# Unordered scatters, weight casts issued turn by turn, and two additions moved from VectorE to TensorE

## The chip, the cores and the metric

The kernel runs on one core of a Trainium2 chip. The metric is the device time of one execution in microseconds (us). Each core has five engines with in-order instruction streams: TensorE (PE; its weight loads are listed as PEld), VectorE (DVE), ScalarE (ACT), GpSimd (POOL) and SyncE (SP). Here SP issues the plain DMAs, POOL the casting and the indirect ones. Data live in DRAM, in SBUF (128 partitions) and in PSUM, the only place that TensorE writes.

## The reference

Two stages. First, a gated linear recurrence with a complex state over 768 steps, for 4 batches and 8 heads of 48 dimensions; its output is then fed, regrouped as 3072 tokens of 384 numbers, to a mixture of eight experts of which each token uses one.

```python
mag = np.sqrt(a_re * a_re + a_im * a_im)
scale = np.minimum(mag, 0.999) / (mag + 1e-06)
a_re_n, a_im_n = (a_re * scale, a_im * scale)
for t in range(S):
    new_re = ar * S_re - ai * S_im          # ar, ai: a_re_n, a_im_n of step t
    new_im = ar * S_im + ai * S_re
    S_re, S_im = (new_re + kv, new_im)      # kv: outer product of k and v of step t
    y[:, :, t] = np.einsum('bhd,bhde->bhe', q[:, :, t], S_re)

logits = x @ w_gate + modality_bias[modality_id]
e_idx = np.argmax(logits, axis=1)           # gate_w: softmax weight of e_idx
for e in range(E):
    mask = e_idx == e
    h = np.maximum(x[mask] @ w1[e], 0.0)
    out[mask] = gate_w[mask, None] * (h @ w2[e])
```

## The kernel before

The sequence is cut into 8 pieces of 96 steps. Four batches x eight heads x eight pieces are 256 rows, handled in two rounds (r = 0, 1) of 128 rows, one row to a partition.

**`elem(r)`** makes what depends on the gates alone. It walks the 96 steps of all 128 pieces backwards, in 12 chunks of 8 steps (c = 11 down to 0). The product of the gates from a step to the end of its piece is the tile `e`. One step is a multiplication on DVE (`x`, L143) and an addition on DVE (`e`, L150) that gives the next `e`; the eight steps of a chunk depend on one another. Between these steps, the list `beside` places pieces of two generators:

- `modulus` (for the chunk two further on): two loads `ab` (a_re, a_im), their squares on ACT (`sq`, L69), the sum of the two squares on DVE (`m`, L72), then Ln, Exp and a Copy on ACT (`m`, `g`, L73 to L76), and the product `g` on DVE (L78). `gates` then makes the scaled gates `an` (DVE L85, ACT L86, L87).
- `hats` (for the chunk just done): the squares of `e` on ACT (`sqe`, L97), their sum on DVE (`me`, L100), Ln and Exp on ACT (L101, L102), the product `qc` on DVE (L104), the product `Qh` on DVE (L107), eight transposes on TensorE (`tq`, L111) that ACT copies to `QT` (L112), and the product of `e` and `kc` on DVE (L114), which goes to DRAM as `kh`.

**`units(r)`** is the matmul part: 16 units a round (8 pieces x 2 batches). A unit loads `KW` (from `kh`) and `V`, transposes (`tk` L177, copied to `KT`), multiplies `wp` (L184, float32, masked into `KW` on DVE, L185), transposes the decayed state (`tz` L207, copied to `Zs` on ACT), multiplies `py` (L219, L223), computes the logits (`lg_ps` L237) and writes the rows of x as bf16. POOL zeroes the padding of `V` and `KT` for each unit (L170, L173), and the load of `V` is queued on SP behind that zeroing.

`elem(0)` runs alone; then `units(0)` and `elem(1)` are interleaved piece by piece; then `units(1)` runs alone. The framework that lowers the program reorders each engine's instructions by its own estimate of when they are ready; from then on each engine runs its list in order.

**`cast_weights`** issues 16 DMAs on POOL (L289, L290) at the start of the program. Each reads one expert's w1 or w2 as float32 (1.57 MB) and writes a bf16 copy of it to DRAM.

**`moe_sorted`** sorts the tokens by expert and handles tiles of 256 slots, each of one expert: 12 tiles at least, and as many of 7 more as the counts need. For each tile, `fetch` loads the expert's two bf16 weight arrays (SP; `w1t`, `w2t`, three buffers each) and gathers the token rows with two indirect DMAs on POOL (`xg`, L449, six buffers); `turn` transposes them (`xg_ps` L457, copied by DVE to `xgT`); `up` multiplies (`h_ps` L469, evacuated in turn by DVE L471 and ACT L473); `down` multiplies (`y_ps` L481), scales the result into `y_sb` (ACT L484 and DVE L486, four buffers) and writes it to the token rows of `out` with two indirect DMAs on POOL (the scatters, L487). The framework takes two scatters to the same tensor as a write after a write, so that each waits until the one before has landed.

Of the kernel before, what the change touches and what calls it, by code (L numbers as in the profile page):

```python
# [19 lines left out]
ET = mybir.EngineType  # L20


def gate_loop(nc, ctx, tc, cpool, ident, identb, q, k, v, a_re, a_im, wgp, x_rows, lg):


    B, H, S, D = q.shape
    L = 96
    G = S // L
    P = 128
# [4 lines left out]
    T = 8  # L34
# [5 lines left out]
    ps = ctx.enter_context(tc.psum_pool(name="aps", bufs=1))  # L40
# [19 lines left out]

    for_round = {}

    def modulus(r, c, box):

        ab = st.tile([P, 2, T, D], F32, name="ab", bufs=3)
        nc.sync.dma_start(out=ab[:, 0], in_=rows(a_re, r, c))
        nc.sync.dma_start(out=ab[:, 1], in_=rows(a_im, r, c))
        sq = st.tile([P, 2, T, D], F32, name="sq")
        nc.scalar.activation(sq[:], ab[:], Act.Square)  # L69
        yield  # L70
        m = st.tile([P, T, D], F32, name="m", bufs=3)
        nc.vector.tensor_tensor(m[:], sq[:, 0], sq[:, 1], Alu.add)  # L72
# [17 lines left out]
    def hats(r, c, e, QT):  # L90

        qc = st.tile([P, T, D], F32, name="qc")
        kc = st.tile([P, T, D], F32, name="kc")
        nc.sync.dma_start(out=qc[:], in_=rows(q, r, c))
        nc.sync.dma_start(out=kc[:], in_=rows(k, r, c))
        sq = st.tile([P, T, 2, D], F32, name="sqe", tag="sq")
        nc.scalar.activation(sq[:], e[:], Act.Square)  # L97
        yield
        m = st.tile([P, T, D], F32, name="me", tag="m", bufs=3)
        nc.vector.tensor_tensor(m[:], sq[:, :, 0], sq[:, :, 1], Alu.add)  # L100
        nc.scalar.activation(m[:], m[:], Act.Ln)  # L101
# [5 lines left out]
        nc.vector.tensor_tensor(Qh[:], e[:], both(qc), Alu.mult)  # L107
        for t4 in range(0, T, 4):
            tp = ps.tile([C, 4, P], F32, name="tq", tag="tp", bufs=2)
            for i in range(4):  # L110
                nc.tensor.transpose(tp[:, i, :], Qh[:, t4 + i].rearrange("p c d -> p (c d)"), ident[:])  # L111
            nc.scalar.copy(QT[:, :, c * T + t4:c * T + t4 + 4], tp.rearrange("c t p -> c p t"))  # L112
        yield
        nc.vector.tensor_tensor(e[:], e[:], both(kc), Alu.mult)  # L114
        nc.sync.dma_start(out=kh[r, :, c * T:(c + 1) * T], in_=e.rearrange("p t c d -> p t (c d)"))

    def elem(r):

        QT = qt.tile([C, P, L], F32, name="QT", bufs=2)
        for_round[r] = QT  # L120
        last = NCH - 1
        E = {last: st.tile([P, T, 2, D], F32, name="e", bufs=3)}
        nc.vector.memset(E[last][:, T - 1, 0, :], 1.0)
        nc.vector.memset(E[last][:, T - 1, 1, :], 0.0)
        cl = un.tile([P, 2, D], F32, name="cl", bufs=1)
        box = {}
        for c in (last, last - 1):
            for _ in modulus(r, c, box):
                pass
        gates(last, box)  # L130
        for c in range(last, -2, -1):
            hs = hats(r, c + 1, E.pop(c + 1), QT) if c < last else iter(())
            ms = modulus(r, c - 2, box) if c > 1 else iter(())
            next(hs, None)
            next(ms, None)
            beside = [None, hs, ms, hs, hs, ms, hs, ms]
            if c >= 0:
                an = box.pop(c)
                if c:
                    E[c - 1] = st.tile([P, T, 2, D], F32, name="e", bufs=3)  # L140
                for i in range(T - 1, -1, -1):
                    x = st.tile([P, 2, 2, D], F32, name="x")
                    nc.vector.tensor_tensor(x[:], E[c][:, i, :, None, :].broadcast_to([P, 2, 2, D]), an[:, i].rearrange("p (u w) d -> p u w d", u=2), Alu.mult)  # L143
# [6 lines left out]
                    nc.vector.tensor_tensor(to, x[:, 0], x[:, 1], Alu.add)  # L150
# [132 lines left out]
def cast_weights(nc, moe_w1, moe_w2):  # L283

    E, Dt, F = moe_w1.shape
    w1b = nc.dram_tensor("w1b", (E, 128, Dt // 128, F), BF16, kind="Internal").ap()
    w2b = nc.dram_tensor("w2b", (E, 128, F // 128, Dt), BF16, kind="Internal").ap()
    for e in range(E):
        nc.gpsimd.dma_start(out=w1b[e], in_=moe_w1[e].rearrange("(k p) f -> p k f", p=128))  # L289
        nc.gpsimd.dma_start(out=w2b[e], in_=moe_w2[e].rearrange("(c p) d -> p c d", p=128))  # L290
    return w1b, w2b


def moe_sorted(nc, ctx, tc, cpool, identb, lg, x_rows, w1b, w2b, moe_modality_id, moe_modality_bias, out):

    N, Dt = out.shape
# [140 lines left out]
    ids = mp.tile([128, NH], U32, name="ids")  # L437
# [38 lines left out]
    def down(i, w2t, hT):  # L476
        for s in range(HS):
            c = i * HS + s
# [3 lines left out]
            y_sb = fp.tile([128, Dt], F32, name="y_sb", bufs=4)  # L482
            if s % 2 == 0:
                nc.scalar.activation(y_sb[:], y_ps[:], Act.Copy, scale=inv[:, 1, c:c + 1])  # L484
            else:
                nc.vector.tensor_scalar(y_sb[:], y_ps[:], inv[:, 1, c:c + 1], None, Alu.mult)  # L486
            nc.gpsimd.indirect_dma_start(out=out, out_offset=bass.IndirectOffsetOnAxis(ap=ids[:, c:c + 1], axis=0), in_=y_sb[:], in_offset=None, bounds_check=N - 1, oob_is_err=False)  # L487


    got = fetch(0)  # L490
# [18 lines left out]
def kernel(  # L509
# [14 lines left out]
    nc = tc.nc  # L524
# [19 lines left out]
    w1b, w2b = cast_weights(nc, moe_w1, moe_w2)  # L544
    with ExitStack() as gstack:
        gate_loop(nc, gstack, tc, cpool, ident, identb, q, k, v, a_re, a_im, wgp, x_rows, lg)
    moe_sorted(nc, ctx, tc, cpool, identb, lg, x_rows, w1b, w2b, moe_modality_id, moe_modality_bias, out)


# [28 lines left out]
```

## Time and profile before

| what | us |
|---|---|
| median of three timed runs (612.57, 619.71, 619.93) | 619.71 |
| the profiled execution's own time | 614.6 |
| its span | 612.7 |
| TensorE busy (matmul), of the span | 397.7 |
| VectorE busy, of the span | 354.4 |
| ScalarE busy, of the span | 266.7 |
| GpSimd busy, of the span | 82.7 |

The mean granted TensorE clock of the profiled execution is 0.851. A profile line of a timeline gives start (us), length (us), engine, line, operation, the tile written and the tiles read, shape and count; in square brackets stands the idle time of that engine before it and what ended it. A float32 matmul of the program appears as two MATMUL records (512 products `wp` are 1024 records), a transpose as one.

### The profile page before, as it was taken

The numbers are of one execution on the slowest core, as the hardware profiler recorded it, in microseconds if no ns is written. First come the engines' busy times: TensorE is split into PE (matmuls) and PEld (weight loads), VectorE is DVE, ScalarE is ACT, GpSimd is POOL, SyncE is SP. The second block draws the span as 40 slices with busy tenths as digits, with TensorE's granted clock in tenths as the row PEclk, the third lists the DMA queues.
The fourth block names the chain that finished last, engine by engine and source line by source line (L and its number), as shares of the span: only waits on it lengthen the run. The fifth ranks groups of instructions, "written<-read, shape, count | busy, mean of one in ns | idle before, by whom it ended". The sixth has DMA issues, their size and how long they took to land. (4 is left out here: it accounts for less than half of the span.)

```text
span 612.7 us, 10055 instructions
## 1 busy us (share of the span) xinstructions
PE 397.7 (65%) x3656; PEld 292.1 (48%) x3656; DVE 354.4 (58%) x884; ACT 266.7 (44%) x597; POOL 82.7 (13%) x144
## 2 busy tenths in 40 slices
PE   0022122129799978987987999999914695876670
PEld 0011011117566656665656767776604574654450
DVE  1899999988876587588871444444365142232120
ACT  3556756475745574476652444444410031211120
POOL 5112000000000000000000000000000343435322
PEclk9999999999755685588996999999955599887886
DMA  9999998365652364353525445444217177765610
GB/s 201 234 243 267 261 254 218 116 175 117 172 151 74 93 159 127 87 154 99 134 70 114 88 93 105 91 98 99 50 12 305 32 269 254 255 230 184 206 53 28
DMA packets 108405, 91.49 MB, mean 149 GB/s; under 512 B 73342, under 2 KB 97314, under 8 KB 108352
## 3 DMA queue, kind: packets, MB, share of 16 engines
q1 hardware_dynamic: 93920, 70.94, 41.7%
q0 software_dynamic: 14432, 19.86, 15.7%
q8 instruction: 31, 0.51, 0.4%
q14 instruction: 22, 0.18, 0.1%
HBM read 86.75 MB, written 29.59 MB: 190 GB/s over the span
## 5 line engine op out<-in xcount | busy, mean ns | idle before, releaser
L111 PE MATMUL tq<-ident,Qh 128*96 128x128 f32 x192 | 42.9, 390 | 119.2 <-DVE Qh L107 119.2
L111 PEld LDWEIGHTS tq<-ident,Qh 128*96 128x96 f32 x192 | 31.3, 180 | 128.2 <-ACT g L76 62.0
L219 PE MATMUL py<-KW,V 96*64 96x192 f32 x512 | 88.9, 378 | 0.0
L185 DVE TENSOR_TENSOR KW<-wp,mask 96x384 f32<-96x384 f32 x64 | 35.3, 553 | 78.5 <-PE wp L184 67.0
L143 DVE TENSOR_TENSOR x<-e,an 128x192 f32<-128x192 f32 x192 | 67.7, 353 | 2.5
L184 PE MATMUL wp<-QT,KT 96*64 96x96 f32 x1024 | 65.8, 287 | 0.8 <-ACT KT L178 0.5
L184 PEld LDWEIGHTS wp<-QT,KT 96*64 96x64 f32 x1024 | 58.5, 165 | 5.6 <-ACT KT L178 4.3
L469 PE MATMUL h_ps<-xgT,w1t 128*128 128x256 bf16 x312 | 42.6, 296 | 25.2 <-DVE hT L471 22.0
L473 ACT ACTIVATE hT<-h_ps 128x512 bf16<-128x512 f32 x26 | 15.5, 597 | 97.5 <-PE h_ps L469 97.5
L150 DVE TENSOR_TENSOR e<-x 128x96 f32<-128x96 f32 x190 | 48.0, 253 | 2.7
L469 PEld LDWEIGHTS <-w1t 128*128 128x128 bf16 x312 | 32.8, 105 | 33.3 <-issue 26.3
L173 POOL MEMSET KT<- 96x256 f32 x32 | 10.9, 365 | 275.0 <-PE wp L184 275.0
L223 PE MATMUL py<-QT,Zs 96*48 96x96 f32 x448 | 37.5, 272 | 14.1 <-ACT Zs L209 14.1
L177 PE MATMUL tk<-ident,KW 96*96 96x96 f32 x256 | 40.1, 298 | 9.4 <-DMA KW<-kh 8.9
L219 PEld LDWEIGHTS py<-KW,V 96*64 96x64 f32 x512 | 39.6, 154 | 10.4 <-issue 2.4
L486 DVE TENSOR_SCALAR y_sb<-y_ps,inv 128x384 f32<-128x384 f32 x13 | 8.0, 617 | 60.9 <-DMA out_dram<-y_sb,ids 48.0
L112 ACT COPY QT<-tq 96x512 f32<-96x512 f32 x48 | 27.5, 582 | 34.9 <-PE tq L111 34.7
L481 PE MATMUL y_ps<-w2t,hT 128*128 128x384 bf16 x208 | 40.5, 353 | 0.0
L223 PEld LDWEIGHTS py<-QT,Zs 96*48 96x48 f32 x448 | 26.7, 136 | 26.9 <-ACT Zs L209 22.7
L209 ACT COPY Zs<-tz 96x512 f32<-96x512 f32 x28 | 16.3, 582 | 48.5 <-PE tz L207 48.5
L177 PEld LDWEIGHTS tk<-ident,KW 96*96 96x96 f32 x256 | 28.5, 154 | 17.6 <-issue 10.4
L178 ACT COPY KT<-tk 96x384 f32<-96x384 f32 x64 | 29.2, 477 | 16.9 <-PE tk L177 16.1
(120 smaller groups left out, 700.6 us busy)
## 6 DMA issues: line engine op xcount, KB each, us to landing
w1t<-w1b SPq DMA_DIRECT2D x13, 768.0 KB, 5.0
w2t<-w2b SPq DMA_DIRECT2D x13, 768.0 KB, 5.5
kh<-e SPq DMA_DIRECT2D x24, 384.0 KB, 2.9
KW<-kh SPq DMA_DIRECT2D x32, 288.0 KB, 3.7
w1b<-in_moe_w_dram POOLq DMA_DIRECT2D x8, 768.0 KB, 43.8
w2b<-in_moe_w_dram POOLq DMA_DIRECT2D x8, 768.0 KB, 46.4
cB<-c_scr SPq DMA_DIRECT2D x56, 96.0 KB, 3.4
ab<-in_a_re_dram SPq DMA_DIRECT2D x24, 192.0 KB, 5.3
```

The source lines that it names most:

```text
L111: nc.tensor.transpose(tp[:, i, :], Qh[:, t4 + i].rearrange("p c d -> p (c d)"), ident[:])
L112: nc.scalar.copy(QT[:, :, c * T + t4:c * T + t4 + 4], tp.rearrange("c t p -> c p t"))
L143: nc.vector.tensor_tensor(x[:], E[c][:, i, :, None, :].broadcast_to([P, 2, 2, D]), an[:, i].rearrange("p (u w) d -> p u w d", u=2), Alu.mult)
L150: nc.vector.tensor_tensor(to, x[:, 0], x[:, 1], Alu.add)
L177: nc.tensor.transpose(tp[:, i, :], KW[:, h4 + i, 0:C], ident[:L, :L])
L178: nc.scalar.copy(KT[:, h4:h4 + 4, 0:L], tp[:])
L184: nc.tensor.matmul(wp[u * 64:(u + 1) * 64, i, :], KT[:, h4 + i, u * 64:(u + 1) * 64], QT[:, p, :], start=True, stop=True)
L185: nc.vector.tensor_tensor(KW[:, h4:h4 + 4, C:], wp[0:L], mask[:, None, :].broadcast_to([L, 4, L]), Alu.mult)
L219: nc.tensor.matmul(py[u * 64:(u + 1) * 64, i, :], V[:, 2 * j + u, :], KW[:, 2 * j + u, :], start=True, stop=(g == 0))
L223: nc.tensor.matmul(py[u * 64:u * 64 + D, i, C:], Zs[:, j, u * 64:u * 64 + D], QT[:, p, :], start=False, stop=True)
L469: nc.tensor.matmul(h_ps[:, f, :], w1t[:, k, ff * 128:(ff + 1) * 128], xgT[:, k, :], start=(k == 0), stop=(k == KD - 1))
L481: nc.tensor.matmul(y_ps[:], hT[:, f, s * 128:(s + 1) * 128], w2t[:, f, :], start=(f == 0), stop=(f == NF - 1))
```

## The change

Three edits.

1. **Sums on TensorE.** The two additions L72 and L100 go. In their place a function `total` adds the two halves of the squares with two accumulating float32 matmuls against the 128x128 identity, into a PSUM tile of 128x384 that shares its two buffers with `wp` (tag "wp"). The Ln on ACT then reads PSUM in place of SBUF.
2. **Casts turn by turn.** The 16 casts are kept in a list. `elem` issues one of them at the end of a chunk, with a dependency on the last addition of that chunk on DVE: ten in round 0 (c = 9 to 0), six in round 1 (c = 11 to 6). They stay on POOL.
3. **Scatters.** Each scatter to `out` is declared independent of the other scatters.

```diff
+    def total(x, y):
+        out = ps.tile([P, T, D], F32, name="total", tag="wp", bufs=2)
+        nc.tensor.matmul(out[:], ident[:], x, start=True, stop=False)
+        nc.tensor.matmul(out[:], ident[:], y, start=False, stop=True)
+        return out[:]
...
         m = st.tile([P, T, D], F32, name="m", bufs=3)
-        nc.vector.tensor_tensor(m[:], sq[:, 0], sq[:, 1], Alu.add)
-        nc.scalar.activation(m[:], m[:], Act.Ln, scale=1.0 / (0.999 * 0.999))
+        nc.scalar.activation(m[:], total(sq[:, 0], sq[:, 1]), Act.Ln, scale=1.0 / (0.999 * 0.999))
...
         m = st.tile([P, T, D], F32, name="me", tag="m", bufs=3)
-        nc.vector.tensor_tensor(m[:], sq[:, :, 0], sq[:, :, 1], Alu.add)
-        nc.scalar.activation(m[:], m[:], Act.Ln)
+        nc.scalar.activation(m[:], total(sq[:, :, 0], sq[:, :, 1]), Act.Ln)
...
-                    nc.vector.tensor_tensor(to, x[:, 0], x[:, 1], Alu.add)
+                    done = nc.vector.tensor_tensor(to, x[:, 0], x[:, 1], Alu.add)
+                if casts and (r or c < last - 1):
+                    cast = casts.pop(0)()
+                    tc.add_manual_dep(cast.ins, done.ins.name, ...)
...
+    casts = []
     for e in range(E):
-        nc.gpsimd.dma_start(out=w1b[e], in_=moe_w1[e].rearrange("(k p) f -> p k f", p=128))
-        nc.gpsimd.dma_start(out=w2b[e], in_=moe_w2[e].rearrange("(c p) d -> p c d", p=128))
+        casts.append(lambda e=e: nc.gpsimd.dma_start(out=w1b[e], in_=...))
+        casts.append(lambda e=e: nc.gpsimd.dma_start(out=w2b[e], in_=...))
...
-            nc.gpsimd.indirect_dma_start(out=out, out_offset=..., in_=y_sb[:], ...)
+            sc = nc.gpsimd.indirect_dma_start(out=out, out_offset=..., in_=y_sb[:], ...)
+            tc.declare_no_dep(sc.ins, group="scatter", reason="rows of different tokens")
+            tc.add_to_no_dep_group("scatter", sc.ins)
```

The order of the instructions changes with it. On DVE, one chunk of `elem(0)` from the first step on, before (the numbers tell one buffer of a tile from another):

```order
L143 TENSOR_TENSOR x_260<-e_191,an_194 128x192
L100 TENSOR_TENSOR me_269<-sqe_252 128x384
L150 TENSOR_TENSOR e_191<-x_260 128x96
L72 TENSOR_TENSOR m_276<-sq_257 128x384
L143 TENSOR_TENSOR x_267<-e_191,an_194 128x192
L150 TENSOR_TENSOR e_191<-x_267 128x96
L104 TENSOR_TENSOR qc_248<-qc_248,me_269 128x384
L143 TENSOR_TENSOR x_274<-e_191,an_194 128x192
L107 TENSOR_TENSOR Qh_289<-e_144,qc_248 128x768
L150 TENSOR_TENSOR e_191<-x_274 128x96
L78 SCALAR_TENSOR_TENSOR g_280<-m_276,g_280 128x384
```

The same stretch of a chunk on DVE now:

```order
L148 TENSOR_TENSOR x_473<-e_399,an_402 128x192
L155 TENSOR_TENSOR e_399<-x_473 128x96
L148 TENSOR_TENSOR x_480<-e_399,an_402 128x192
L155 TENSOR_TENSOR e_399<-x_480 128x96
L148 TENSOR_TENSOR x_489<-e_399,an_402 128x192
L155 TENSOR_TENSOR e_399<-x_489 128x96
L148 TENSOR_TENSOR x_500<-e_399,an_402 128x192
L109 TENSOR_TENSOR qc_461<-qc_461,me_482 128x384
L155 TENSOR_TENSOR e_399<-x_500 128x96
L112 TENSOR_TENSOR Qh_506<-e_326,qc_461 128x768
L148 TENSOR_TENSOR x_504<-e_399,an_402 128x192
L84 SCALAR_TENSOR_TENSOR g_497<-m_491,g_497 128x384
```

The two additions are gone; `qc` now stands behind three whole steps and the `x` of a fourth, where it stood behind two steps. In both, the gates `an` of the next chunk stand ahead of the first row.

On TensorE, in the interleaved stage, from the transposes `tz` of a unit to its first logits, before:

```order
L207 MATMUL tz_1536<-ident_58,Z_1492 96x128 x4
L223 MATMUL py_1546<-QT_106,Zs_1541 48x96 x2
L219 MATMUL py_1546<-KW_1333,V_1334 64x192 x2
L223 MATMUL py_1546<-QT_106,Zs_1541 48x96 x2
L223 MATMUL py_1558<-QT_106,Zs_1541 48x96 x2
L237 MATMUL lg_ps_1406<-yT_1544,wgp_66 32x96 x2
```

The same place of a unit now (`sqe` and `sq` are the squares of `e` and of the gates):

```order
L216 MATMUL tz_1870<-ident_58,Z_1826 96x128 x4
L66 MATMUL total_1944<-sqe_1926,ident_58 128x384
L67 MATMUL total_1944<-sqe_1926,ident_58 128x384
L232 MATMUL py_1880<-QT_90,Zs_1875 48x96 x2
L228 MATMUL py_1880<-KW_1662,V_1663 64x192 x2
L66 MATMUL total_1953<-sq_1931,ident_58 128x384
L246 MATMUL lg_ps_1735<-yT_1878,wgp_66 32x96 x2
```

The first sum now stands between `tz` and the `py` that waits for `Zs`, and the first half of the second between the last `py` and the logits.

More of the change, by code (lines that the diff above doesn't have):

```diff
@@ L20, with gate_loop @@
 ET = mybir.EngineType
-def gate_loop(nc, ctx, tc, cpool, ident, identb, q, k, v, a_re, a_im, wgp, x_rows, lg):
+def gate_loop(nc, ctx, tc, cpool, ident, identb, q, k, v, a_re, a_im, wgp, x_rows, lg, casts):
     B, H, S, D = q.shape
@@ L149, in elem @@
                     to = E[c][:, i - 1] if i else (E[c - 1][:, T - 1] if c else cl[:])
-                    nc.vector.tensor_tensor(to, x[:, 0], x[:, 1], Alu.add)
+                    done = nc.vector.tensor_tensor(to, x[:, 0], x[:, 1], Alu.add)
+                if casts and (r or c < last - 1):
+                    cast = casts.pop(0)()
+                    tc.add_manual_dep(cast.ins, done.ins.name, mybir.DependencyInfo(mybir.DependencyClass.Sync, mybir.DependencyReason.DATA), reason="spreads the casts over the turns")
             for g in (ms, hs):
@@ L542 @@
         nc.sync.dma_start(out=wgp[u * 64:u * 64 + D, :, 0:E], in_=moe_w_gate.rearrange("(j u d) e -> u d j e", u=2, d=D)[u])
[L544 removed]
+    w1b, w2b, casts = cast_weights(nc, moe_w1, moe_w2)
     with ExitStack() as gstack:
[L546 removed]
+        gate_loop(nc, gstack, tc, cpool, ident, identb, q, k, v, a_re, a_im, wgp, x_rows, lg, casts)
     moe_sorted(nc, ctx, tc, cpool, identb, lg, x_rows, w1b, w2b, moe_modality_id, moe_modality_bias, out)
```

6 lines of the change are left out of this document (4 added, 2 removed).

## The prediction

> **What bounds the kernel now.** I read the stages first, then what waits in each. Busy time by stage; columns after the stretch: length, then PE, PEld, DVE, ACT and POOL busy with instruction counts, granted clock, DMA share, GB/s. The bounds are the first step of `elem(0)`, its end, the end of `elem(1)`, the end of the units, and the first expert matmul.
>
> ```profile
> 18.70:126.00 107.30, 21.05 (x88) 15.99 (x88) 100.86 (x268) 63.14 (x115) 7.11 (x12) 1.00 1.00 227
> 126.00:302.00 176.00, 144.94 (x1267) 104.06 (x1267) 134.47 (x356) 107.08 (x248) 6.93 (x27) 0.74 0.50 128
> 302.00:446.00 144.00, 131.66 (x1639) 97.39 (x1638) 63.12 (x154) 64.49 (x180) 9.15 (x38) 0.96 0.41 88
> ...
> 488.00:612.70 124.70, 84.34 (x592) 60.25 (x592) 31.47 (x51) 22.97 (x39) 47.10 (x48) 0.84 0.54 183
> ```
>
> `elem(0)` is bound by DVE (100.86 of 107.30 us). The interleaved stage has PE at 82% and DVE at 76%. The units alone are PE's: 144 us for 18 units, 8.0 each. In the expert stage no engine is full, so its waits decide. What waits there (waiter, whom for, us, times, longest):
>
> ```profile
> DVE y_sb L486 <- DMA out_dram<-y_sb,ids: 48.0, 8, 9.0
> POOL out_dram L487 <- DMA out_dram<-y_sb,ids: 30.9, 10, 5.8
> ```
>
> DVE stands 48 us before `y_sb`, because the scatter that reads that buffer has not landed; and POOL stands 31 us before a scatter for the one ahead of it. While DVE stands, `hT` isn't evacuated and PE stops as well.
>
> **The scatters.** TensorE's `down` of tiles 0, 1 and 12, then a gather of POOL and its last scatter, then the DMA in 494 to 514 us:
>
> ```profile
> 492.55 2.76 PE L481 MATMUL y_ps<-w2t,hT 128*128 128x384 bf16 x16
> 498.11 2.76 PE L481 MATMUL y_ps<-w2t,hT 128*128 128x384 bf16 x16
> ...
> 594.75 2.76 PE L481 MATMUL y_ps<-w2t,hT 128*128 128x384 bf16 x16
> ```
>
> ```profile
> 485.40 0.95 POOL L449 DMA_INDIRECT xg<-x_rows,idg  x1 [0.30 <-issue]
> ...
> 606.49 0.97 POOL L487 DMA_INDIRECT out_dram<-y_sb,ids  x1 [1.94 <-DMA out_dram<-y_sb,ids]
> ```
>
> ```profile
> DMA packets 1388, 6.54 MB, mean 327 GB/s; under 512 B 216, under 2 KB 280, under 8 KB 1385
> ```
>
> With nothing in the way a tile takes 498.11 - 492.55 = 5.56 us on PE; over the twelve steps to tile 12 it took (594.75 - 492.55) / 12 = 8.5. What is late next? POOL issues four indirect DMAs a tile at about 0.95 + 0.30 = 1.25 us: 5.0 us, just under PE. The DMA moves 1.57 MB of weights, 0.2 of gathers and 0.39 of scatters a tile (from the shapes); at the 327 GB/s of those 20 us that is 6.6 us. But two pairs of weight arrays have a head start, and at that rate of the DMA tiles 0 and 1 still came 5.56 apart, so 6.6 is a ceiling. I take 5.75 a tile: `down` of tile 12 starts at 492.55 + 12 x 5.75 = 561.6, ends 2.8 later, its scatter is issued by 565, and from the last issue to the end it is 612.7 - 606.5 = 6.2: end at 571, **41 us earlier**. Ends: 5.56 gives 44, 6.6 gives 31.
>
> **The casts.** In `elem(0)` the DMA engines are full (share 1.00), yet DVE is 94% busy: loads are issued a chunk ahead. Only the start shows them.
>
> ```profile
> ACT sq L69 <- DMA ab<-in_a_im_dram: 11.2, 4, 6.4
> ```
>
> Without casts the first of these waits (6.4 us) shrinks, but three sums of 2.6 us (below) now precede the first step, at 18.7 before. I take 3 us gained (0 to 7). Paced, a cast a chunk leaves DMA less loaded; in `elem(1)` six casts fall on a share of 0.50. On POOL the padding of `V` and `KT` queues behind a cast that waits for DVE, and SP's load of `V` behind that; a unit's own DVE work stands in DVE's list behind the same chunk, so I cost it at nothing; if the order slips, it is one late load a chunk, 6 x the 6.4 us above at the very most.
>
> **The sums, price of one.** DVE first, in a chunk of `elem(0)`: steps with the two additions, and steps without.
>
> ```profile
> 60.92 0.36 DVE L143 TENSOR_TENSOR x<-e,an 128x192 f32<-128x192 f32 x1
> 61.31 0.26 DVE L150 TENSOR_TENSOR e<-x 128x96 f32<-128x96 f32 x1
> 61.60 0.36 DVE L143 TENSOR_TENSOR x<-e,an 128x192 f32<-128x192 f32 x1
> ...
> 63.55 0.95 DVE L85 TENSOR_TENSOR an<-ab,g 128x768 f32<-128x768 f32 x1
> 64.42 0.35 DVE L143 TENSOR_TENSOR x<-e,an 128x192 f32<-128x192 f32 x1
> 64.68 0.55 DVE L100 TENSOR_TENSOR me<-sqe 128x384 f32<-128x384 f32 x1
> 65.15 0.25 DVE L150 TENSOR_TENSOR e<-x 128x96 f32<-128x96 f32 x1
> 65.32 0.55 DVE L72 TENSOR_TENSOR m<-sq 128x384 f32<-128x384 f32 x1
> 65.79 0.35 DVE L143 TENSOR_TENSOR x<-e,an 128x192 f32<-128x192 f32 x1
> ```
>
> From `x` to `x` it is 1.37 us with both additions and 0.68 without. Two additions of 0.55 thus cost only 0.69: they fill the gap in which a dependent step waits for the one before. That is all that DVE saves in a chunk.
>
> PE's price must come from other shapes. Transposes: two runs in `elem(0)`, two in the interleaved stage's slow part, one in its fast part; then the group of 18 to 126 us, with the mean of one:
>
> ```profile
> 68.31 1.92 PE L111 MATMUL tq<-ident,Qh 128*96 128x128 f32 x8 [7.30 <-DVE Qh L107]
> 77.52 1.91 PE L111 MATMUL tq<-ident,Qh 128*96 128x128 f32 x8 [7.30 <-DVE Qh L107]
> ...
> 162.66 1.94 PE L111 MATMUL tq<-ident,Qh 128*96 128x128 f32 x8 [3.69 <-DVE Qh L107]
> ...
> 176.70 1.94 PE L111 MATMUL tq<-ident,Qh 128*96 128x128 f32 x8
> ...
> 217.31 1.08 PE L111 MATMUL tq<-ident,Qh 128*96 128x128 f32 x8 [0.56 <-DVE Qh L107]
> ```
>
> and their group:
>
> ```profile
> L111 PE MATMUL tq<-ident,Qh 128*96 128x128 f32 x88 | 21.0, 420 | 102.9 <-DVE Qh L107 102.9
> ```
>
> Eight take 1.92 us and one lasts 0.42, so they follow each other by (1.92 - 0.42) / 7 = 0.214 (1.67 ns a column); at 217 us, in proportion, by 0.214 x 1.08 / 1.92 = 0.120 (0.94 ns). The clock column shows 1.00 in `elem(0)`, but the rows there are as slow as those at 162 us, where it shows 0.50: the array runs at half speed in `elem(0)`. A float32 matmul is two records, so a sum is four passes of 384 columns: 4 x 0.64 = **2.57 us slow, 1.44 fast**. The nearest dense row, `down` above, takes at most 2.76 / 16 = 0.17 for a pass of 384 bf16 columns: four such passes are 0.7 fast, 1.4 slow, my lower end. I take the float32 rows, since the data are float32; nothing there hints at more.
>
> **`elem(0)`, a chunk.** The squares of `e` on ACT are below. Time 0 is the start of `an` (63.55). The chunk is 77.52 - 68.31 = 9.21 us long.
>
> ```profile
> 62.97 0.84 ACT L97 ACTIVATE sqe<-e 128x768 f32<-128x768 f32 x1 [1.35 <-DVE e L150]
> ```
>
> and the group of the Ln, which stands here for Exp and Copy too:
>
> ```profile
> L101 ACT ACTIVATE me<-me 128x384 f32<-128x384 f32 x24 | 12.3, 514 | 0.9 <-DVE me L100 0.9
> ```
>
> The squares end at 0.26. The first sum is done at 0.3 + 2.57 + 0.2 (the tail of a pass, 0.42 - 0.21) = 3.1, Ln and Exp at 4.2. `Qh` and `kc` have the shape of `an` (0.87 to the next start), `qc` and `g` that of `me` (0.47, or 0.26 and 0.17 for the `x` and `e` around them). DVE gets to `qc` in its new place at 0.87 + 3 x 0.68 + 0.26 = 3.2 and waits 1.0. The second sum is done at 5.65, its Ln, Exp and Copy at 7.2; DVE gets to `g` at 4.2 + 0.47 + 0.17 + 0.87 + 0.26 = 6.0 and waits 1.2. The rest of the chunk is 0.47 + 0.17 + 0.87 and three steps, less 0.1 at the seam: **10.6 us, 1.4 more**. Nine chunks have both sums (13 us); the last two only the first (1 us). Less the 3 us of the start: +11, and **+10** if some second sums run partly fast. Ends: no wait left, 11 x -0.69 and the start at 7: -15; start at 0: +14.
>
> **Interleaved stage.** Two stretches of it, same columns as above:
>
> ```profile
> 162.00:211.00 49.00, 46.33 (x335) 33.29 (x336) 32.46 (x89) 25.30 (x55) 1.84 (x7) 0.50 0.46 122
> 211.00:225.00 14.00, 10.63 (x129) 7.44 (x128) 13.10 (x37) 10.53 (x25) 0.71 (x3) 0.99 0.50 137
> ```
>
> Slow, PE is full: a round is 176.70 - 162.66 = 14.0 us. Two sums add 5.1, less about 0.7 that PE idles a round (2.67 over 3.5), which the first sum now fills: 18.4. Fast, DVE is the full one. PE's work in a fast round becomes 14/13 units (32 less the 18 later) of 8.0, 1.1 of transposes and 2.9 of sums: 12.6; DVE's shrinks by about 1. So 12.6. Before, 13 rounds take 176. With nine fast and four slow: 9 x 12.6 + 4 x 18.4 = 187, **+11**. Why more fast rounds than now? The row at 162.66 shows PE empty for 3.69 us before a slow stretch; sums fill such gaps.
>
> **The sum.** Span 612.7 + 10 + 11 - 41 = 592.7; with the 1.9 us around it 594.6 against the 614.6 of that execution. The median, 619.71, lies 0.8% above; the three runs lie on both sides. Scaled, 594.6 would be 599.5; I predict between, 597.
>
> **Rivals.** 2% (607.3 to 632.1) is about what a measurement tells from no change.
>
> *PE stays slow through the interleaved stage* (other side). Place: the PE list, each sum ahead of `py`. 13 x 18.4 = 239, +63; `elem(0)` +14; scatters -41: 651. With `elem(0)` at +10 it outweighs the scatters once fewer than six of 13 rounds are fast (the stage at 207). For it: 0.50 held from 162 to 211 with PE busy 95%. Against: the sums are the densest work on PE. Chance 0.13.
>
> *The sums release the clock everywhere.* `elem(0)` at 8.5 a chunk and a shorter start, -10; 13 x 12.6, -12; -41: 552. For it: 211 us shows that dense work does it. [...] Against: in `elem(0)` PE is empty or transposing for the other half of a chunk, and the rows there are slow in every chunk. Chance 0.10.
>
> *DMA takes over*, full with weights and scatters at once: 6.6 us a tile (-31), six rounds slow (+23), `elem(0)` +10: 617. For it: 327 GB/s with only four scatters in those 20 us. Against: 5.56 a tile there. Chance 0.18.
>
> *The scatters stay in order in effect*, held by four `y_sb` buffers or by POOL: +21 and no gain, 636. Against: both waits shown above are on scatters that hadn't landed, and the buffers come free with them. Chance 0.04.
>
> My forecast keeps 0.55, with a range of its own of 577 to 612. Of it 0.5 is faster by over 2%; with 0.10 of the second rival and a little of the third: faster 0.63, same 0.23, slower 0.14. Range: 560 to 628, which leaves out most of the second rival and the first.
>
> **What would show it.** Right: no wait of DVE's `y_sb` on `out_dram` over 2 us, `down` every 5.6 to 6 us; in `elem(0)`, DVE waiting before `qc` and `g` for ACT, chunks of 10 to 11 us; `total` records near 0.9 us there. Wrong: chunks under 9.2 us or `total` at half that; rounds over 16 us; tiles over 6.6 us with the DMA share at 1.

## The result, and the profile after

The kernel after takes **565.0 us** (median of four runs, 562.6 to 569.0) against 619.8 before: ratio **0.914, interval 0.906 to 0.922**. Faster, as forecast, by more than twice the gain: 54.8 us where I had 23. The profiled execution is the longest of the four (568.95 us, span 567.2). Where TensorE's clock moves about among the units, executions of one kernel differ by 10 us and more (one without sums took 564.9 us at a mean clock of 0.88 and 582.4 at 0.84); ratios and intervals below compare undisturbed executions on both sides, medians are over all.

Stages after; columns as in the prediction (length, PE, PEld, DVE, ACT, POOL busy, granted clock, DMA share, GB/s). The bounds are the first step of `elem(0)`, its last (`cl`), the first `tk` of `units(0)`, the first `tk` of `units(1)`, the end of the units; then the first `h_ps` and the end.

```profile
15.44:127.00 111.56, 59.97 (x168) 32.59 (x168) 93.85 (x248) 61.91 (x115) 7.19 (x9) 0.71 0.78 180
127.00:143.70 16.70, 8.37 (x25) 4.66 (x26) 10.41 (x24) 10.69 (x22) 0.85 (x1) 0.70 1.00 201
143.70:322.90 179.20, 160.83 (x1581) 109.08 (x1582) 132.15 (x344) 108.27 (x262) 12.88 (x38) 0.93 0.67 154
322.90:441.20 118.30, 111.13 (x1400) 83.14 (x1400) 48.81 (x117) 50.49 (x145) 8.00 (x33) 0.96 0.41 85
...
483.40:567.20 83.80, 73.55 (x592) 55.43 (x589) 32.72 (x51) 23.08 (x39) 46.70 (x48) 0.95 0.74 273
```

The second and third of these stretches before:

```profile
126.00:138.80 12.80, 1.91 (x8) 1.46 (x9) 11.40 (x25) 9.91 (x21) 0.00 (x0) 1.00 0.67 162
138.80:328.00 189.20, 163.85 (x1497) 116.99 (x1498) 137.39 (x368) 111.20 (x262) 8.15 (x32) 0.75 0.47 122
```

The stretch among the units shrank by 10 us although TensorE got the sums to do: its clock is 0.93 in place of 0.75. The column is too high where it shows 1.00 beside slow rows, as it does in `elem(0)` of before (eight `tq` in 1.92 us there, in 1.94 at 0.50 and in 1.08 at 0.99) and still in the first 11 us of this stretch, where `wp` lasts 368 ns against 246 a little later:

```profile
138.80:149.90 11.10, 10.85 (x95) 9.69 (x96) 8.56 (x22) 6.92 (x16) 0.61 (x2) 1.00 0.51 112
149.90:328.00 178.10, 153.00 (x1404) 107.30 (x1402) 128.83 (x347) 104.28 (x247) 7.54 (x30) 0.74 0.47 122
L184 PE MATMUL wp<-QT,KT x64: 367/368/423, 140.5 to 147.8; 96*64 96x96 f32 x64
L184 PE MATMUL wp<-QT,KT x32: 246/246/297, 155.4 to 156.7; 96*64 96x96 f32 x32
```

(The `wp` lines give the shortest, median and longest in ns, and the first and last start.) An estimate: the column stands at 0.50 from 162 to 211 us of before and at 1.00 from 212 to 224; if a clock between them is a mix of these two, 2 x (1 - clock) of the time is at half. With those 11 us counted as half speed that is 55% of the stretch before; after, where the rows agree with the column, 14%. The way there (`cl` to the first `tk`) grew by 4 us. I call 143.7 to 322.9 "the stretch" from here on; it isn't the prediction's interleaved stage, which ran from `cl` to 302 us, 1.9 us behind a `tk` of before that now starts at 296.3.

The expert stage, TensorE's `down` of tiles 0, 1 and 12 after:

```profile
487.66 2.76 PE L491 MATMUL y_ps<-w2t,hT 128*128 128x384 bf16 x16
493.21 2.76 PE L491 MATMUL y_ps<-w2t,hT 128*128 128x384 bf16 x16
...
555.33 2.76 PE L491 MATMUL y_ps<-w2t,hT 128*128 128x384 bf16 x16
```

and two of its waits (waiter, whom for, us, times, longest):

```profile
DVE y_sb L496 <- PE y_ps L491: 27.6, 13, 2.6
...
POOL out_dram L498 <- ACT y_sb L494: 9.1, 3, 3.3
```

`down` comes every (555.33 - 487.66) / 12 = 5.64 us, most of them 5.55 apart. Nobody waits for an earlier scatter; DVE now waits for TensorE, as it should where TensorE sets the pace. The stage takes 83.8 us in place of 124.4.

`elem(0)`: one chunk after, from one square of `e` to the next (start, length):

```profile
68.29 0.84 ACT L103 ACTIVATE sqe<-e 128x768 f32<-128x768 f32 x1 [1.95 <-DVE e L155]
...
69.19 0.94 PE L66 MATMUL total<-sqe,ident 128*128 128x384 f32 x2 [3.57 <-ACT sqe L103]
...
69.94 1.47 PE L67 MATMUL total<-sqe,ident 128*128 128x384 f32 x2
...
71.20 1.48 PE L66 MATMUL total<-sq,ident 128*128 128x384 f32 x2
...
72.48 1.25 PE L67 MATMUL total<-sq,ident 128*128 128x384 f32 x2
72.52 0.56 DVE L109 TENSOR_TENSOR qc<-qc,me 128x384 f32<-128x384 f32 x1 [0.38 <-ACT me L107]
...
75.40 0.56 DVE L84 SCALAR_TENSOR_TENSOR g<-m,g 128x384 f32<-128x384 f32 x1 [0.99 <-ACT g L82]
...
78.27 0.84 ACT L103 ACTIVATE sqe<-e 128x768 f32<-128x768 f32 x1 [1.95 <-DVE e L155]
```

The waits forecast before `qc` and `g` are there (0.38 and 0.99; I had 1.0 and 1.2), and the chunk is 9.98 us. Each sum takes neither 2.57 nor 1.44 us but something between (71.20 - 69.19 = 2.0): within a chunk the clock comes and goes (the column shows 0.80 from 69.1 to 70.5 us, 0.50 to 71.2 and 0.59 to 73.8).

### The profile page after: what moved, and what is told of

It is laid out like the page before. It is cut to its first block, busy times and chain, and to the rows that moved or that the text cites. A ratio compares the mean times of both kernels' runs of the same rounds, so it can differ in the third digit from the quotient of the medians.

```text
span 567.2 us, 10405 instructions
## 1 busy us (share of the span) xinstructions
PE 436.7 (77%) x3848; PEld 303.1 (53%) x3848; DVE 341.8 (60%) x836; ACT 263.3 (46%) x597; POOL 81.7 (14%) x144
## 5 line engine op out<-in xcount | busy, mean ns | idle before, releaser
L228 PE MATMUL py<-KW,V 96*64 96x192 f32 x512 | 81.0, 350 | 0.0
L193 PE MATMUL wp<-QT,KT 96*64 96x96 f32 x1024 | 57.4, 264 | 2.2 <-ACT KT L187 1.2
L66 PE MATMUL total<-sqe,ident 128*128 128x384 f32 x48 | 26.8, 647 | 40.3 <-ACT sqe L103 40.3
L155 DVE TENSOR_TENSOR e<-x 128x96 f32<-128x96 f32 x190 | 48.5, 255 | 10.2 <-DMA kh<-e 5.9
L193 PEld LDWEIGHTS wp<-QT,KT 96*64 96x64 f32 x1024 | 50.7, 147 | 6.5 <-ACT KT L187 5.2
L186 PE MATMUL tk<-ident,KW 96*96 96x96 f32 x256 | 34.5, 268 | 12.9 <-DMA KW<-kh 9.8
L116 PE MATMUL tq<-ident,Qh 128*96 128x128 f32 x192 | 28.0, 294 | 16.3 <-DVE Qh L112 16.3
L479 PE MATMUL h_ps<-xgT,w1t 128*128 128x256 bf16 x312 | 37.7, 279 | 1.1 <-DVE xgT L469 1.1
L116 PEld LDWEIGHTS tq<-ident,Qh 128*96 128x96 f32 x192 | 21.9, 136 | 28.5 <-issue 13.6
L491 PE MATMUL y_ps<-w2t,hT 128*128 128x384 bf16 x208 | 35.9, 326 | 0.0
L186 PEld LDWEIGHTS tk<-ident,KW 96*96 96x96 f32 x256 | 24.6, 137 | 20.8 <-issue 11.4
L238 ACT COPY yT<-py 128x192 f32<-128x192 f32 x64 | 20.5, 320 | 30.2 <-DVE state L237 25.0
```

Source lines behind the costliest of these rows:

```text
L66: nc.tensor.matmul(out[:], ident[:], x, start=True, stop=False)
L155: done = nc.vector.tensor_tensor(to, x[:, 0], x[:, 1], Alu.add)
L186: nc.tensor.transpose(tp[:, i, :], KW[:, h4 + i, 0:C], ident[:L, :L])
L193: nc.tensor.matmul(wp[u * 64:(u + 1) * 64, i, :], KT[:, h4 + i, u * 64:(u + 1) * 64], QT[:, p, :], start=True, stop=True)
L228: nc.tensor.matmul(py[u * 64:(u + 1) * 64, i, :], V[:, 2 * j + u, :], KW[:, 2 * j + u, :], start=True, stop=(g == 0))
L479: nc.tensor.matmul(h_ps[:, f, :], w1t[:, k, ff * 128:(ff + 1) * 128], xgT[:, k, :], start=(k == 0), stop=(k == KD - 1))
```

## The experiments

**Theory 1**: in the stretch among the units the sums release TensorE's clock; they cost time in `elem(0)`, where DVE waits for them. **Theory 2**: the paced casts opened the stretch, and the sums only cost. **Theory 3**: DVE's relief (two additions fewer a chunk) is what counts.

### Each part alone

Free scatters alone:

```diff
-            nc.gpsimd.indirect_dma_start(out=out, ...)
+            sc = nc.gpsimd.indirect_dma_start(out=out, ...)
+            tc.declare_no_dep(sc.ins, group="scatter", reason="rows of different tokens")
+            tc.add_to_no_dep_group("scatter", sc.ins)
```

> The kernel before with one part of the change: the scatters of the expert stage are declared independent of each other; casts and sums as before. Both theories give this part the expert stage and nothing else: from the first h_ps to the end 83.8 us, as after the whole change, against 124.4 before, so 40 us less: about 579 us, ratio 0.935. The stages ahead of it stay as before (first h_ps at 488 to 489 us). If the scatters gain only beside the other two parts, it is above 590.

581.7 us median; ratio 0.930 (0.917 to 0.942). Its expert stage, from the first `h_ps` to the end:

```profile
501.40:586.10 84.70, 74.35 (x591) 55.87 (x589) 32.69 (x51) 23.08 (x39) 46.80 (x48) 0.94 0.74 270
```

84.7 us in place of 124.4: the scatters' gain needs no other part of the change. Its first `h_ps` came 13 us later than expected, though nothing ahead of it differs from before: in this execution, the longest of the four, the stretch took 198.5 us where before has 189.2. A stretch without sums varies by that much by itself.

The sums alone:

```diff
-        nc.vector.tensor_tensor(m[:], sq[:, 0], sq[:, 1], Alu.add)
-        nc.scalar.activation(m[:], m[:], Act.Ln, scale=1.0 / (0.999 * 0.999))
+        nc.scalar.activation(m[:], total(sq[:, 0], sq[:, 1]), Act.Ln, scale=1.0 / (0.999 * 0.999))
...
-        nc.vector.tensor_tensor(m[:], sq[:, :, 0], sq[:, :, 1], Alu.add)
-        nc.scalar.activation(m[:], m[:], Act.Ln)
+        nc.scalar.activation(m[:], total(sq[:, :, 0], sq[:, :, 1]), Act.Ln)
```

> The kernel before with one part of the change: the sums of squares on TensorE; casts and scatters as before. The stretch in dispute runs from the first tk of units(0) to the first tk of the second round's units alone: 189.2 us at a granted clock of 0.75 before, 179.2 at 0.93 after. Theory 1, the sums release the clock there: this stretch takes 176 to 182 us at 0.9 or more; elem(0) and its end are 5 to 9 us longer, so the time is 612 to 620. Theory 2, the casts did it and the sums only cost: the stretch is 189 us or longer at 0.8 or less, and the time 625 to 640.

609.8 us; ratio 0.989 (0.980 to 0.998). The casts alone:

```diff
+                if casts and (r or c < last - 1):
+                    cast = casts.pop(0)()
+                    tc.add_manual_dep(cast.ins, done.ins.name, ...)
```

> The kernel before with one part of the change: a cast of weights behind each chunk instead of all at the start; sums and scatters as before. Theory 1 (the sums release the clock): the start is 3 us shorter, the stretch from the first tk to the units alone stays near 189 us at a clock near 0.75, and the time is 615 to 620. Theory 2 (the casts did it): the stretch is near 179 us at 0.9 or more, and the time 603 to 609.

622.9 us, where before, beside it, had 616.3; no interval. The stretch with the sums alone:

```profile
148.60:318.40 169.80, 154.73 (x1581) 106.21 (x1582) 131.85 (x343) 107.58 (x262) 8.18 (x32) 0.96 0.53 136
```

and with the casts alone:

```profile
134.00:319.00 185.00, 158.71 (x1496) 113.39 (x1496) 135.75 (x364) 110.21 (x261) 12.84 (x38) 0.88 0.66 150
```

The sums alone make the stretch 169.8 us at 0.96, the shortest so far. With the casts alone it is 185.0, where theory 2 wanted 179, and the 0.88 is again too high: up to 180.2 us the column shows 1.00 beside slow rows.

```profile
133.90:180.20 46.30, 41.89 (x301) 30.46 (x302) 30.47 (x79) 26.41 (x62) 4.08 (x10) 1.00 0.80 166
180.20:319.00 138.80, 116.87 (x1197) 83.02 (x1196) 105.38 (x286) 83.82 (x200) 8.75 (x28) 0.84 0.62 145
L188 PE MATMUL wp<-QT,KT x128: 364/367/423, 135.4 to 170.2; 96*64 96x96 f32 x128
```

With those 46 us counted as half speed, 49% of the stretch is at half, close to the 55% of before; with the sums alone it is 8%. So the casts didn't release the clock here, and their 4 us less than before lie within what a stretch without sums varies by (198.5 above). The end of `elem(0)` is the first start of `cl` (of two), before:

```profile
L150 DVE TENSOR_TENSOR cl<-x x2: 258/259/260, 125.6 to 315.1; 128x96 f32<-128x96 f32 x2
```

after:

```profile
L155 DVE TENSOR_TENSOR cl<-x x2: 252/255/258, 126.7 to 293.6; 128x96 f32<-128x96 f32 x2
```

with the sums alone:

```profile
L155 DVE TENSOR_TENSOR cl<-x x2: 247/252/257, 131.4 to 288.6; 128x96 f32<-128x96 f32 x2
```

and with the casts alone:

```profile
L150 DVE TENSOR_TENSOR cl<-x x2: 258/258/259, 119.5 to 306.0; 128x96 f32<-128x96 f32 x2
```

So up to `cl` the sums cost 131.4 - 125.6 = 5.8 us, the casts gain 6.1, and both together (+1.1 after) nearly add up. From `cl` to the first `tk` the sums cost again: 17.2 us with the sums alone, 14.5 with the casts alone, 13.2 before.

The change without the sums (those of the gates; the squares of `e` in the same way):

```diff
-        nc.scalar.activation(m[:], total(sq[:, 0], sq[:, 1]), Act.Ln, scale=1.0 / (0.999 * 0.999))
+        nc.vector.tensor_tensor(m[:], sq[:, 0], sq[:, 1], Alu.add)
+        nc.scalar.activation(m[:], m[:], Act.Ln, scale=1.0 / (0.999 * 0.999))
...
```

> The kernel after with the sums of squares back on VectorE: free scatters and paced casts only. Theory 1 (the sums release the clock): the stretch from the first tk to the units alone is near 189 us at a clock near 0.75, elem(0) is 4 us shorter than after, and the time is 570 to 577, slower than after by 1 to 2%. Theory 2 (the casts did it, the sums only cost): the stretch is 179 us or less and the time 555 to 561, faster than after.

570.8 us; ratio 0.922 (0.911 to 0.932): the time of theory 1, but its interval overlaps that of after. The stretch, in the longest of the five executions (589.0 us), is longer than theory 1 had it (189 us):

```profile
133.90:338.40 204.50, 183.62 (x1497) 131.15 (x1498) 137.09 (x364) 111.57 (x262) 12.87 (x38) 0.65 0.59 136
```

Both kernels once more, side by side:

> Free scatters and paced casts without the sums, beside the kernel after on one chip. If the sums gain more among the units than the 5.8 us that they cost in elem(0): this one is slower than after by 4 to 15 us, 569 to 580. If gain and cost cancel: within 3 us of after, 563 to 569.

> The kernel after, beside the one without sums on one chip: 563 to 568 us. Its stretch from the first tk to the units alone took 179.2 and 174.7 us so far; 174 to 180 expected.

571.8 without the sums, ratio 0.929 (0.923 to 0.935); 566.7 with them, 0.926 (0.921 to 0.931). The medians differ by 5 to 6 us in both pairs (in the first they did not run side by side), the intervals overlap in both. The stretch without the sums took 197.9 us at 0.72 in the second of them, that with the sums 171.7 at 0.96; but the two executions without sums that were profiled were among the longer ones. With all of them in place, as the change has them, the sums bring 0 to 6 us.

### Where the sums count

Sums on TensorE in `elem(1)` alone (for `elem(0)` alone the condition is turned round); then sums in `elem(1)` that nobody reads, while VectorE adds. Shown for the gates:

```diff
+        if r:
             nc.scalar.activation(m[:], total(sq[:, 0], sq[:, 1]), Act.Ln, scale=...)
+        else:
+            nc.vector.tensor_tensor(m[:], sq[:, 0], sq[:, 1], Alu.add)
+            nc.scalar.activation(m[:], m[:], Act.Ln, scale=...)
```

```diff
+        if r:
+            total(sq[:, 0], sq[:, 1])
+        nc.vector.tensor_tensor(m[:], sq[:, 0], sq[:, 1], Alu.add)
+        nc.scalar.activation(m[:], m[:], Act.Ln, scale=...)
```

> After, but with the sums of squares on TensorE in elem(1) alone; in elem(0) VectorE adds, as before. Theory 1 (the sums that stand among the units release the clock): elem(0) is as with paced casts and no sums (cl at 119.5 us, first tk near 134), and the stretch from the first tk to the units alone is 170 to 182 us at a clock of 0.9 or more: 553 to 560 us in all, faster than after (565). Rival (the sums of elem(0) leave the clock high, and it stays so): the stretch is 185 us or longer at 0.88 or less, and the time 563 to 585.

> After, but with the sums of squares on TensorE in elem(0) alone. Theory 1 (the sums that stand among the units release the clock): the stretch from the first tk to the units alone is as without sums, 185 to 205 us at 0.65 to 0.88, the first tk as after at 143.7, so 571 to 592 us, slower than after. Rival (the sums of elem(0) leave the clock high): the stretch is near 179 us and the time 562 to 569, as after.

> As the kernel with the sums in elem(1) alone, but VectorE adds in elem(1) too: TensorE makes the same sums there and nobody reads them. Theory 1 (the clock, by denser work on TensorE): the stretch from the first tk to the units alone is 170 to 185 us at 0.9 or more, and the time within 1% of that of the kernel with the sums in elem(1). Rival (VectorE's relief of 0.7 us a chunk, or the order in which ACT gets the sums): the stretch is 185 to 205 us, as without sums, and the time 563 to 589.

With the sums in `elem(1)` alone: 556.2 us, ratio 0.905 (0.900 to 0.909); one of its six executions took 1249.9 us, for a reason that I don't know, and the median of the other five is 555.2. In `elem(0)` alone: 585.9, no interval. Unread in `elem(1)`: 555.7, ratio 0.890 (0.881 to 0.899). The stretches, in this order (the second in the longest of its four executions):

```profile
133.90:303.00 169.10, 154.66 (x1580) 105.90 (x1581) 132.66 (x348) 108.55 (x262) 12.87 (x38) 0.96 0.74 165
145.80:344.20 198.40, 176.57 (x1497) 125.07 (x1498) 136.34 (x365) 110.54 (x262) 12.83 (x38) 0.67 0.61 140
133.10:304.90 171.80, 162.80 (x1580) 111.35 (x1581) 136.64 (x368) 109.74 (x262) 12.81 (x38) 0.90 0.70 160
```

Theory 1 holds in all three. Sums in `elem(0)` are a loss: they didn't carry the clock into the stretch (0.67). And sums that nobody reads, beside additions that DVE still makes, are worth no less than sums that are read (555.7 and 556.2 us, against 570.8 and 571.8 without any sums). That ends theory 3: what the sums bring is the clock. (The framework's order of instructions shifts a little with each of these edits; no run separates that from the clock.)

The sums and the scatters, with the casts at the start:

```diff
-                if casts and (r or c < last - 1):
+                if False:
...
+    for cast in casts:
+        cast()
```

> After, but with all casts issued at the start: scatters and sums only. If the paced casts gain their 5 us at the start and cost nothing among the units: first x at 18.7, first tk at 148.5, the stretch as after (near 179), about 570 us. If the casts that fall on elem(1) cost there what they gain at the start (the stretch took 179.2 us after, and 169.8 with the sums alone): the stretch is near 170 and the time 560 to 566, as after.

572.6 us, ratio 0.930 (0.927 to 0.933), and the stretch:

```profile
147.20:316.50 169.30, 154.66 (x1580) 106.24 (x1581) 131.77 (x343) 107.32 (x261) 8.15 (x32) 0.96 0.52 136
```

Both parts of the two expectations mixed: the stretch is near 170 and the time is 572. To see whether the 179.2 of after is its own, it ran again, beside the kernel with the sums in `elem(1)` alone:

> The kernel after, once more, beside the others of this call. Its stretch from the first tk to the units alone took 179.2 us, that of the same kernel with all casts at the start 169.3, and that with the sums in elem(1) alone 169.1. If the casts in elem(1) hold it up each time: 176 to 182 again. If it was that one execution: nearer 170. About 565 us.

> The kernel with the sums of squares on TensorE in elem(1) alone, once more, on the chip of the others of this call: 553 to 559 us, some 1.5% under after; if its lead lay in the chip, no difference to after.

565.8 us (0.922, 0.912 to 0.933) and 549.5 us (0.897, 0.888 to 0.906). Their stretches took 174.7 and 168.2 us, and that of the third run of after 171.7. So 5 to 8 us of the 179.2 come and go, and 2 to 5 more than with the casts at the start remain. Moving the sums of `elem(0)` back to VectorE is a gain of its own, 16 us here; of the 14.8 in the two spans 6.2 are made by `cl`, 1.6 from there to the first `tk`, 6.4 in the stretch. Why the stretch gains too I haven't taken apart.

### What a sum costs there

Each sum of `elem(1)` made twice, the first unread:

```diff
         if r:
+            total(sq[:, 0], sq[:, 1])
             nc.scalar.activation(m[:], total(sq[:, 0], sq[:, 1]), Act.Ln, scale=...)
```

> The sums in elem(1) alone, and each of them made twice there, once unread: the price of two more sums of 1.29 us a chunk while the clock is high. If a fast round is bound by TensorE, as my forecast took it (14/13 units, the transposes and the sums in a row): 12 x 2.6 = 31 us more in that stretch, 200 us, 587 in all. If the sums fill gaps that TensorE has beside VectorE: 0 to 10 us more, 556 to 566.

590.5 us, ratio 0.965 (0.959 to 0.971). The stretch:

```profile
132.90:337.00 204.10, 184.32 (x1665) 121.76 (x1666) 139.63 (x360) 110.77 (x266) 12.77 (x38) 0.96 0.61 138
```

36 us more than the 168.2 beside it, at the same clock, 29.5 of them in TensorE's busy time: at this point TensorE is the bound of a round, as my forecast had it. So half of the sums might do: in `elem(1)` those of `e` alone, with the gates' back on VectorE, or the other way round.

```diff
-        if r:
-            nc.scalar.activation(m[:], total(sq[:, 0], sq[:, 1]), Act.Ln, scale=...)
-        else:
-            nc.vector.tensor_tensor(m[:], sq[:, 0], sq[:, 1], Alu.add)
-            nc.scalar.activation(m[:], m[:], Act.Ln, scale=...)
+        nc.vector.tensor_tensor(m[:], sq[:, 0], sq[:, 1], Alu.add)
+        nc.scalar.activation(m[:], m[:], Act.Ln, scale=...)
```

> In elem(1) only the squares of e are summed on TensorE; those of the gates are added by VectorE, as in elem(0). If one sum a chunk is enough to release the clock: 0.93 or more, and TensorE is freed of 12 x 1.29 us (half of the 36 us that doubling cost is 18): the stretch takes 150 to 156 us against 168, and the time is 531 to 538. If one is not enough: below 0.9, 180 us or longer, 560 or more.

> In elem(1) only the squares of the gates are summed on TensorE; those of e are added by VectorE. As for the squares of e alone: 150 to 156 us and 531 to 538 if one sum a chunk releases the clock; 180 us or longer and 560 or more if it takes two in a row.

548.8 us, ratio 0.892 (0.872 to 0.912), and 549.7, ratio 0.882 (0.849 to 0.916): neither expectation, and no different from both sums (549.5, on another chip). The stretch with the squares of `e` alone (in the shortest of its four executions), its first `wp`, and the stretch with those of the gates alone:

```profile
133.20:297.50 164.30, 142.58 (x1545) 99.99 (x1545) 131.73 (x353) 107.62 (x262) 12.84 (x38) 1.00 0.76 170
L198 PE MATMUL wp<-QT,KT x64: 364/367/422, 134.6 to 141.9; 96*64 96x96 f32 x64
...
134.20:304.70 170.50, 151.42 (x1533) 106.32 (x1534) 133.05 (x359) 108.89 (x262) 12.81 (x38) 0.88 0.72 163
```

In the first the column shows 1.00 throughout, though its first 11 us are slow as well: 7% of the stretch at half, as with both sums. One sum a chunk released the clock there (32 `wp` take 1.54 us from 153.0, 2.83 in those 11), and still the stretch is only 4 us shorter than with both: TensorE stands 21.7 us. With the gates' sums alone, in one of the longer of four executions, the clock was 0.88. So the second sum was nearly free and the third and fourth cost 36: TensorE becomes the bound at about two sums a chunk.

### What releases the clock

Unread sums as above, each made of eight matmuls of 96 columns in place of two of 384:

```diff
+    def short(x, y):
+        out = ps.tile([P, T, D], F32, name="total", tag="wp", bufs=2)
+        for t in range(0, T, 2):
+            nc.tensor.matmul(out[:, t:t + 2], ident[:], x(t), start=True, stop=False)
+            nc.tensor.matmul(out[:, t:t + 2], ident[:], y(t), start=False, stop=True)
```

> As the kernel with unread sums in elem(1) (VectorE adds everywhere in it), but each unread sum is made of eight matmuls of 96 columns in place of two of 384: the same operands and columns, more loads of weights, TensorE as full or fuller. If a high share of busy time releases the clock: 0.90 or more, the stretch from the first tk to the units alone 170 to 185 us, and the time 550 to 565. If it takes long streams: the clock is as without sums, 0.65 to 0.88, the stretch 195 us or longer with the added work, and the time 575 or more.

558.1 us, ratio 0.906 (0.887 to 0.925). The stretch:

```profile
133.80:312.50 178.70, 165.70 (x1832) 134.34 (x1833) 139.08 (x374) 109.05 (x262) 12.82 (x38) 0.94 0.71 156
```

With streams of 96 columns the clock is 0.94, where it was 0.65 to 0.88 in the runs without sums in `elem(1)`. It didn't take long ones.

The same idea where nothing else is in play: the routing stage, where TensorE stands 14.26 us and then makes the 64 matmuls of `inv_ps`. Unread matmuls, on top of the sums in `elem(1)` alone; first 26 and 12 of 256 columns, then 38 ahead and 10 on `onlo`, which DVE finishes some 4 us before `inv_ps` may start. The diff of the second:

```diff
+    def warm(n, w, x):
+        box = pp.tile([128, Dt], F32, name="warm", tag="y", bufs=2)
+        for _ in range(n):
+            nc.tensor.matmul(box[:, 0:x.shape[-1]], w, x, start=True, stop=True)
+    warm(38, io128[:], seg0.rearrange("p e t -> p (e t)"))
...
+    warm(10, onlo[:, 0], onlo[:, 0:2].rearrange("p t x -> p (t x)"))
```

> The sums in elem(1) alone, and in the routing stage 26 unread float32 matmuls of 256 columns ahead of inv_ps, where TensorE stands 14.26 us, and 12 behind it. Theory 1 (slow rows are a matter of the clock, and work that nobody reads mends it): the 64 matmuls of inv_ps take 7 us in place of 13.9 and the first 24 of h_ps 2.8 in place of 4.2: 7 to 8.4 us less than without them, about 548. If these rows are slow for another reason (weight loads, the float32 operands): no change, or up to 2 us more where the unread work overlaps.

> The sums in elem(1) alone, with unread matmuls in the routing stage up to the start of inv_ps: 38 on constants, then 10 on onlo, which fill the 3.92 us that were empty ahead of inv_ps in the run with 26 and 12. If only the empty stretch took the clock: the rows of inv_ps are fast from the start, 64 in 7 to 8 us in place of 13.9, and the time 541 to 544 against 549. [...]

549.2 us (0.895, 0.891 to 0.900), no gain; then 542.3 us (0.877, 0.863 to 0.892). TensorE in the first of them, last unread matmuls and `inv_ps`:

```profile
430.74 10.52 PE L394 MATMUL warm<-seg,io 128*128 128x256 f32 x48
445.18 13.90 PE L454 MATMUL inv_ps<-load,onlo 96*128 96x76 f32 x64 [3.92 <-DVE load L451]
```

and in the second:

```profile
429.73 10.52 PE L394 MATMUL warm<-seg,io 128*128 128x256 f32 x48
440.09 4.48 PE L394 MATMUL warm<-onlo 96*128 96x256 f32 x20
444.41 7.26 PE L455 MATMUL inv_ps<-load,onlo 96*128 96x76 f32 x64
```

The framework had moved the twelve that I had put behind `inv_ps` ahead of it, and still 3.92 us stood empty before it: `inv_ps` took 13.90 us as ever. With the gap filled it takes 7.26, and from the first `tk` of `units(1)` to the first `h_ps` it is 153.9 us in place of 160.2. This is the fastest kernel of the study, some 23 us under after (565 to 567).

## Why the prediction was wrong, step by step

| us, profiled executions | forecast | measured |
|---|---|---|
| start and `elem(0)`, to `cl` | +10 | +1.1 |
| interleaved stage | +11 | -4.9 |
| units alone | 0 | -1.1 |
| experts | -41 | -40.6 |
| span | -20 | -45.5 |

**The scatters: right.** -41 forecast, -40.6 here and -39.7 by themselves. That it came so close is luck in part: the stage took 83.1 to 84.7 us in most profiled runs with free scatters, but 88.3 to 88.9 in four that ran together on one chip. A tile is 5.55 us, just under the 5.75 that I took; DMA didn't take over (share 0.74 in the stage), and no wait on `out_dram` is left.

**The interleaved stage: the step that failed is "With nine fast and four slow".** A round at the high clock I priced at 12.6 us, 13 of them 164. With the sums alone the 13 rounds take, on the bounds of that term, 161.8 us (`cl` at 131.4 to 1.9 us behind the `tk` at 291.3): the price was right within 2 us. TensorE is only just the bound there: a third and a fourth sum cost their full time, the second hardly any. How many rounds would be slow I had guessed from before, against my own note that the sums fill the gaps. Four of 18.4 us are 74 of 187 us, 40% of the time; the granted clock says 14% after and 8% where it is 0.96. My second rival had this part (-12, all rounds fast), at a chance of 0.10; I had given it only as a package with a gain in `elem(0)`, which the runs refute. The two belonged apart. Of the 25.5 us by which the span came out shorter than forecast, 16 lie in this stage and 9 in `elem(0)`.

**`elem(0)`: right in kind, too dear.** The waits came where I had put them. But the sums ran partly at the higher clock (0.71 in the mean of `elem(0)`), so the waits were 0.4 and 1.0 us in the chunk shown, and seven chunks in the middle took 10.2 us on average, not 10.6. And in the second chunk of before an addition had held DVE up, for squares of the gates whose load was late, which I had not seen:

```profile
27.40 0.56 DVE L72 TENSOR_TENSOR m<-sq 128x384 f32<-128x384 f32 x1 [1.13 <-ACT sq L69]
...
29.19 0.56 DVE L104 TENSOR_TENSOR qc<-qc,me 128x384 f32<-128x384 f32 x1 [0.68 <-ACT me L102]
```

That chunk took 11.4 us before and 8.5 with the sums alone. By themselves the sums cost 5.8 us here, not 14. The casts gained 6.1, not 3; in the kernel after, 3.3 of it at the first step, as forecast.

**The casts on their way: costed at nothing, which the runs neither refute nor prove.** From `cl` to the first `tk` it takes 3.9 us more after, with a DMA share of 1.00 there; but that is the sums' doing, since it takes as long with the sums alone (17.2 us) and 14.5 with the casts alone. In the stretch after takes two to ten us more than with all casts at the start (171.7 to 179.2 against 169.3); yet with the sums in `elem(1)` alone and the same six casts it takes 168.2 and 169.1, so the casts alone don't explain it, and what does stays open. In `elem(0)` they gain 6.1; the kernel with all casts at the start took 572.6 us, after 565 to 567.

**The rivals.** PE slow throughout (651), DMA taking over (617) and ordered scatters (636) are out by the rows above. The range (560 to 628) held the time; the one that I gave my own forecast (577 to 612) did not.

Of the 45.5 us, then, the scatters are 40; casts and sums share the rest. The sums are an odd edit: in `elem(0)` they cost 6 us and on the way to the first `tk` 4 more, among the units they repay it by the clock alone, and the same clock is to be had without reading them.

## What to carry to other kernels

Where a stretch on TensorE runs at a granted clock well under 1, ask first what keeps it there: here two sums a chunk that nobody read, put among the units, were worth more than the operations they add (555.7 us against 570.8 without any sums), and only two more sums a chunk, with TensorE the bound, cost 36 us. Price a term in both clock states and let the share of each be its own unknown, with its own rival; a package of a likely and an unlikely effect hides the likely one. And a chain of transfers that wait for each other for no reason in the data shows as a wait on the output itself: such a gain came out as read from the waits. Last, check a clock column against the length of rows of one shape: here it showed 1.00 over as much as 46 us of slow rows.

## What the runs showed of the hardware that I had not expected

Unread work changed the speed of what followed: `inv_ps` took 7.26 us in place of 13.90. With 3.92 us empty behind that work it took 13.90 again. And busy time didn't bring the clock back by itself: in before, TensorE is by its records busy with `inv_ps` without a break:

```profile
468.00:482.00 14.00, 13.90 (x64) 13.73 (x64) 0.00 (x0) 0.00 (x0) 0.00 (x0) 0.50 0.23 96
```

13.90 of 14.00 us busy, and the clock is 0.50 throughout, while with the clock high at its start the same 64 matmuls kept it for their 7.26 us:

```profile
444.40:451.70 7.30, 7.27 (x65) 7.11 (x63) 0.00 (x0) 0.00 (x0) 0.00 (x0) 1.00 0.39 161
```

So 13.90 us of busy time in the records didn't release the clock. Nor did the length of the streams or the number of weight loads decide it by itself: sums in streams of 96 columns, with a load to each matmul, released it in the stretch (1833 loads to 1832 matmuls, clock 0.94), while `wp`, with 96 columns too, stayed slow in before (368 ns each, from 140.5 to 147.8 us). The records give 128*128 for the operand that the sums load, 96*64 and 96*128 for `wp` and `inv_ps`; whether that makes the difference stays open, and with it why the rows of before at 162 us, busy 95%, stay at 0.50.
